# The transform along 512 first, in seven products on operands the experts share, then along 2048 in four phases

## The chip, the cores and the metric

The kernel runs on one core of a Trainium2 chip. The metric is the time of one execution on the device, in microseconds; less is better. The five engines of a core have queues of their own: TensorE (PE in the profile) multiplies matrices into eight banks of PSUM, VectorE (DVE) and GpSimd (POOL) add and subtract, ScalarE (ACT) copies, rounds and evaluates functions, SyncE (SP) issues all the DMAs.

## The reference

The result is g * a + (1 - g) * b, row by row of x (2048 rows t, 512 columns). Here a is the real part of a two-dimensional Fourier transform of x, b a mixture of all eight experts with softmax weights, and g a sigmoid of x with a weight vector.

```python
a = jnp.einsum("bsd,ed->bse", x, dft_hid_re)          # along 512
b = jnp.einsum("bsd,ed->bse", x, dft_hid_im)
y = jnp.einsum("ts,bse->bte", dft_seq_re, a) - jnp.einsum("ts,bse->bte", dft_seq_im, b)   # along 2048
...
h = _silu(xf @ w1[e]) @ w2[e]
out = out + w * h                                      # for each of 8 experts
...
return g * a + (1 - g) * b
```

The two transforms may be taken in either order.

## The kernel before

**Splitting.** Every product is computed in float32 on operands that are split into a high part, rounded by ScalarE, and a low part, the difference, made by VectorE (`vt`, L120) or GpSimd (`pt`, L117). One product of tiles is three matmuls of 128x512 (`mm`, L126, L129, L130): high by high, high by low, low by high. `split_at` plans the two steps for one tile, `wide` for a double one of 128x1024.

**Seven products.** A product of two by two blocks is made with seven block products in place of eight. Sums and differences of blocks are the operands; they are numbered 1 to 7. The transforms take them in two halves that fit PSUM: X, products 1, 2 and 5 (six banks), and Y, products 6, 3, 7 and 4 (eight banks).

**Order.** The kernel is a list of events, each with a planned time (`ev`); the list is sorted and the instructions are issued in that order on each engine. `keep_in_program_order` holds it. So what stands ahead on an engine's queue runs first, and waits for its semaphores first.

**The transform before.** It goes along 2048 first. Phases are named by (pr, c, ph): half pr of the output rows, c for the cosine or sine matrix, ph X or Y; there are eight, of NK = 8 steps k each, with 18 matmuls a step in X and 24 in Y, 1344 in all. The right operands come from the matrices (`plan_right`: tiles ca, cb and cd loaded by SP; in a Y step VectorE makes the difference cb, then two sums in ca, then the low parts c73 and c64; in an X step the difference cd and the low parts c12 and c5). The left operands xl come from x (`plan_left_x`, `plan_left_y`: some small sums and three splits per k). Finished blocks go to DRAM (ud), are loaded again, split (`plan_uv`) and multiplied with the 512-long matrices in `y_part`, four groups gi of eight times 12 matmuls, 384. The last group is interleaved with the first step of the experts. `plan_prep_x` makes the operands of the experts from x, beside this stage, and puts them into DRAM (xbd); `load_x` brings them back. The logits of the router are computed in phase (1, 0, X), with splits of their own.

**The experts.** 86 steps follow. A step has seven products m (six matmuls each, banks m_a to m_d) for the first layer and 42 for the second (banks o_a to o_d, one step later); ScalarE copies the first sums out of the bank (`snap`: tiles s, u, p) before the next product adds into the same bank. GpSimd makes the operands of w1 and w2 here.

## Time and profile before

| | us |
|---|---|
| median of three runs | 2090.86 (2092.91, 2090.86, 2090.81) |
| profiled execution, span | 2090.8 |
| TensorE busy | 2055.9 (98%) |
| VectorE busy | 1624.7 (78%) |
| GpSimd busy | 1486.9 (71%) |
| ScalarE busy | 1250.8 (60%) |

The transform takes the first 412 us of the span, the experts the rest. A page of the profile gives the busy time, a list of waits names the engine that ended each idle time, and a timeline has the single instructions. Where an engine is busy it is not shown whether it is at its own pace or is held by something else: this is read from the duration of one instruction.

### The profile page before, as it was taken

Reading aid. Unit: us, or ns where it says so; the run is one execution under the profiler, and the core shown is the slowest. Engines: PE = TensorE matmul, PEld = TensorE weight load, DVE = VectorE, ACT = ScalarE, POOL = GpSimd, SP = SyncE. Lnnn points to the kernel's source line nnn. Section 1 sums busy time; section 2 is a strip of 40 time slices with the busy share of each in tenths; the row PEclk is TensorE's granted clock in tenths of the full one; section 3 lists DMA queues with packets and bytes.
Section 4 is the critical chain, followed back from the end, with each engine's and each line's share of the span. In section 5 each row is a group of like instructions: output and inputs, shape, how many; then the busy total and the mean of one; then the engine's idle time right before and its main releaser. Section 6 shows DMA issues by size and latency. Waiting matters only on the chain.

```text
span 2090.8 us, 26671 instructions
## 1 busy us (share of the span) xinstructions
PE 2055.9 (98%) x9032; PEld 1690.9 (81%) x9032; DVE 1624.7 (78%) x2456; ACT 1250.8 (60%) x2213; POOL 1486.9 (71%) x1371
## 2 busy tenths in 40 slices
...
POOL 0010000459889888898888888888888888888884
...
DMA packets 76129, 235.65 MB, mean 113 GB/s; under 512 B 8372, under 2 KB 8372, under 8 KB 75992
## 3 DMA queue, kind: packets, MB, share of 16 engines
...
q14 instruction: 67, 0.55, 0.1%
...
## 4 chain that ended last, share of the span: by engine, by line
PE 77%; issue 2%; DMA 1%; DVE 1%; POOL 1%; ACT 1%; SPq 0%; POOLq 0%; DVEq 0%; ACTq 0%
PE o_b L126 7%; PE m_b L126 7%; PE o_b L129 7%; PE o_b L130 7%; PE m_b L129 7%; PE m_b L130 7%; PE o_d L126 4%; PE o_d L129 4%; PE o_d L130 4%; PE m_d L126 4%; PE m_d L129 4%; PE m_d L130 4%; PE o_a L129 2%; PE o_a L126 2%; PE o_a L130 2%; PE m_a L129 2%
## 5 line engine op out<-in xcount | busy, mean ns | idle before, releaser
L117 POOL TENSOR_TENSOR w<-w1s,w 128x512 fp32r<-128x512 f32 x258 | 334.7, 1297 | 137.7 <-ACT w L123 137.6
L117 POOL TENSOR_TENSOR w<-w2s,w 128x512 fp32r<-128x512 f32 (+1 forms) x264 | 335.4, 1271 | 37.1 <-ACT w L123 37.0
L120 DVE TENSOR_TENSOR acc<-o_b,acc 128x512 f32<-128x512 f32 x352 | 242.7, 690 | 118.4 <-PE o_b L130 115.7
L126 PE MATMUL m_b<-xb,w 128*128 128x512 f32 x688 | 269.3, 391 | 16.3 <-ACT xb_1w L123 8.4
L126 PE MATMUL o_b<-h,w 128*128 128x512 f32 x688 | 268.1, 390 | 1.9 <-ACT h L123 1.4
L130 PE MATMUL m_b<-xb,w 128*128 128x512 f32 x688 | 268.6, 390 | 0.0
L129 PE MATMUL m_b<-xb,w 128*128 128x512 f32 x688 | 268.6, 390 | 0.0
L129 PE MATMUL o_b<-h,w 128*128 128x512 f32 x688 | 267.7, 389 | 0.0
L130 PE MATMUL o_b<-h,w 128*128 128x512 f32 x688 | 267.7, 389 | 0.0
L123 ACT ACTIVATE w<-w1s 128x512 fp32r<-128x512 f32 x258 | 162.1, 628 | 152.1 <-POOL w1s L117 135.0
L117 POOL TENSOR_TENSOR h<-b,h 128x512 fp32r<-128x512 f32 x172 | 223.5, 1300 | 5.2 <-ACT h L123 5.2
L123 ACT ACTIVATE h<-m_c 128x512 fp32r<-128x512 f32 x172 | 103.1, 600 | 193.8 <-DVE m_c L120 191.0
L117 POOL TENSOR_TENSOR w1s<-w1s 128x256 f32<-128x256 f32 x258 | 192.0, 744 | 6.8
L126 PEld LDWEIGHTS m_b<-xb,w 128*128 128x128 f32 x688 | 129.6, 188 | 45.4 <-issue 8.8
L123 ACT ACTIVATE h<-b 128x512 fp32r<-128x512 f32 x172 | 108.7, 632 | 93.8 <-PE m_d L130 58.5
L123 ACT ACTIVATE w<-w2s 128x512 fp32r<-128x512 f32 (+1 forms) x264 | 162.4, 616 | 2.6 <-POOL w2s L117 2.6
L126 PEld LDWEIGHTS o_b<-h,w 128*128 128x128 f32 x688 | 129.2, 188 | 30.7 <-ACT h L123 1.8
L130 PEld LDWEIGHTS m_b<-xb,w 128*128 128x128 f32 x688 | 129.7, 189 | 27.1
L129 PEld LDWEIGHTS m_b<-xb,w 128*128 128x128 f32 x688 | 129.8, 189 | 26.7
L130 PEld LDWEIGHTS o_b<-h,w 128*128 128x128 f32 x688 | 129.1, 188 | 26.9
L129 PEld LDWEIGHTS o_b<-h,w 128*128 128x128 f32 x688 | 129.1, 188 | 26.5
L120 DVE TENSOR_TENSOR acc<-o_d,acc 128x512 f32<-128x512 f32 x176 | 121.1, 688 | 30.5 <-PE o_d L130 27.9
...
## 6 DMA issues: line engine op xcount, KB each, us to landing
...
```

Of the source, the lines that this page charges most:

```text
L117: pin(nc.gpsimd.tensor_tensor(*a))
L120: pin(nc.vector.tensor_tensor(*a))
L123: pin(nc.scalar.activation(dst, src, f, **kw))
L126: ins = nc.tensor.matmul(ps, lh, rh, start=start, stop=False, skip_group_check=True)
L129: nc.tensor.matmul(ps, lh, rl, start=False, stop=False, skip_group_check=True)
L130: nc.tensor.matmul(ps, ll, rh, start=False, stop=stop, skip_group_check=True)
```

## The change

The transform now goes along 512 first. **Stage one** has the seven products with the experts' own split operands of x (xop, made once, stored to xbd, and used by stage one, by the logits and by the experts) and split operands of the 512-long matrices (wop). It goes over two halves hf of the rows, seven products m in the order 1, 2, 6, 5, 7, 3, 4, four blocks j, six matmuls: 336. `evict1` puts the result into raw tiles, stored to rawd. **Stage two** goes along 2048 with cosine and sine stacked, so that there are four phases (pr, ph), (0, X), (1, X), (1, Y), (0, Y), of 16 steps each: again 1344 matmuls. The left operands come from the raw tiles, and those of the Y phases from rawd. `plan_out_x` and `plan_out_y` gate the result (`gate_y`) and put it into the experts' accumulators or to DRAM (yd); there is no `y_part` and no `plan_prep_x`. The first experts' step follows the last phase with nothing between. Loads of its x operands are planned in the last phase.

Some operations pass to GpSimd: the low parts of xop (but those of product 1), the sums of x of the second half of stage one, left_x for k from 8 on, the three sums and one low part of left_y, the first difference cb of each Y step, and gates.

VectorE in one step of a Y phase, before (names are c, then phase and step; the step is phase (0, 1, Y), k = 5):

```order
L120 TENSOR_TENSOR cb015_1252<-cb015_1252 128x512
L120 TENSOR_TENSOR ca015_1250<-cb015_1252,ca015_1250 128x512
L120 TENSOR_TENSOR ca015_1250<-ca015_1250 128x512
L120 TENSOR_TENSOR c73015l_1299<-cb015_1252,c73015h_1298 128x1024
L120 TENSOR_TENSOR c64015l_1304<-ca015_1250,c64015h_1303 128x1024
```

VectorE in one step of phase (1, Y), k = 6, after:

```order
L121 TENSOR_TENSOR ca1_6_2369<-cb1_6_2371,ca1_6_2369 128x512
L121 TENSOR_TENSOR ca1_6_2369<-ca1_6_2369 128x512
L121 TENSOR_TENSOR xl10_34_2426<-rawy10_2338,xl10_34_2426 128x512
L121 TENSOR_TENSOR c731_6l_2423<-cb1_6_2371,c731_6h_2422 128x1024
L121 TENSOR_TENSOR c641_6l_2432<-ca1_6_2369,c641_6h_2431 128x1024
```

The difference cb is gone from VectorE's step, and the low part of a left operand (xl_34) stands in it.

GpSimd in the whole of the transform before, from its setup to the experts' operands:

```order
L117 TENSOR_TENSOR c73011l_1117<-cb011_1073,c73011h_1116 128x1024
L117 TENSOR_TENSOR c64011l_1123<-ca011_1071,c64011h_1122 128x1024
L117 TENSOR_TENSOR both_81<-ident_78 18x9
L117 TENSOR_TENSOR c12101l_1449<-ca101_1410,c12101h_1448 128x1024
L117 TENSOR_TENSOR c5101_1459<-cd101_1412,c5101_1459 128x512
L117 TENSOR_TENSOR c12111l_2170<-ca111_2133,c12111h_2169 128x1024
L117 TENSOR_TENSOR c5111_2177<-cd111_2135,c5111_2177 128x512
```

GpSimd in phase (1, Y) after, around steps 5 to 7:

```order
L118 TENSOR_TENSOR cb1_5_2320<-cb1_5_2320 128x512
L118 TENSOR_TENSOR xs10_1_2408<-rawy10_2338 128x256
L118 TENSOR_TENSOR xs10_1_2408<-rawy10_2338,xs10_1_2408 128x256
L118 TENSOR_TENSOR cb1_6_2371<-cb1_6_2371 128x512
L118 TENSOR_TENSOR rawy10_2338<-rawy10_2338,xs10_1_2408 128x256
L118 TENSOR_TENSOR xl10_76_2417<-xs10_1_2408,xl10_76_2417 128x512
L118 TENSOR_TENSOR cb1_7_2412<-cb1_7_2412 128x512
```

GpSimd had single low parts at phase changes; it now has a cb in each Y step, and between these the chain xs, xs, rawy, xl_76 of a left operand.

GpSimd in stage one after, in its second half (xo are operands of x by half, product and k; xq, xa sums), where nothing stood before:

```order
L118 TENSOR_TENSOR xo1_2_0_486<-xb10_220,xo1_2_0_486 128x512
L118 TENSOR_TENSOR xo1_8_0_496<-xa10_218,xo1_8_0_496 128x512
L118 TENSOR_TENSOR xq10_503<-xb10_220,xa10_218 128x512
L118 TENSOR_TENSOR xo1_2_1_498<-xb11_221,xo1_2_1_498 128x512
L118 TENSOR_TENSOR xo1_8_1_500<-xa11_219,xo1_8_1_500 128x512
L118 TENSOR_TENSOR xq11_514<-xb11_221,xa11_219 128x512
L118 TENSOR_TENSOR xa10_218<-xa10_218 128x512
L118 TENSOR_TENSOR xa11_219<-xa11_219 128x512
L118 TENSOR_TENSOR xa10_218<-xq10_503,xa10_218 128x512
L118 TENSOR_TENSOR xa11_219<-xq11_514,xa11_219 128x512
L118 TENSOR_TENSOR xo1_6_0_561<-xa10_218,xo1_6_0_561 128x512
L118 TENSOR_TENSOR xo1_6_1_579<-xa11_219,xo1_6_1_579 128x512
```

Eight sums and two low parts stand between the low parts of product 2 and those of product 6 (the third in TensorE's order).

GpSimd after, at the start of the last phase (0, Y):

```order
L118 TENSOR_TENSOR cb0_0_2830<-cb0_0_2830 128x512
L118 TENSOR_TENSOR cb0_1_2872<-cb0_1_2872 128x512
L118 TENSOR_TENSOR c730_1l_2916<-cb0_1_2872,c730_1h_2915 128x1024
L118 TENSOR_TENSOR c640_1l_2922<-ca0_1_2870,c640_1h_2921 128x1024
L118 TENSOR_TENSOR cb0_2_2912<-cb0_2_2912 128x512
L118 TENSOR_TENSOR c211_2967<-c211_2967,gy1_2834 128x1024
L118 TENSOR_TENSOR cb0_3_2964<-cb0_3_2964 128x512
L118 TENSOR_TENSOR c121_2925<-c121_2925,gy1_2834 128x1024
L118 TENSOR_TENSOR p51_2190<-p51_2190,gy1_2834 128x1024
L118 TENSOR_TENSOR cb0_4_3007<-cb0_4_3007 128x512
```

The low parts of step 1 and three gates (c211, c121, p51) stand among the differences cb of steps 0 to 4.

TensorE where the experts begin, before: after product 1 of step 0 (m0_b) the last group of the transform (y3) follows.

```order
L126 MATMUL m0_b_3501<-xb0_1_1_3391,w1_0_12_3314 128x512
L129 MATMUL m0_b_3501<-xb0_1_1_3391,w1_0_12_3314 128x512
L130 MATMUL m0_b_3501<-xb0_1_1_3391,w1_0_12_3314 128x512
L126 MATMUL y3_0_3479<-uv3_0_1_3290,wd0_1_2368 128x512
L129 MATMUL y3_0_3479<-uv3_0_1_3290,wd0_1_2368 128x512
L130 MATMUL y3_0_3479<-uv3_0_1_3290,wd0_1_2368 128x512
```

TensorE there after:

```order
L127 MATMUL u0_41_2956<-c640_15h_3537,xl15_34_2826 128x512
L130 MATMUL u0_41_2956<-c640_15l_3538,xl15_34_2826 128x512
L131 MATMUL u0_41_2956<-c640_15h_3537,xl15_34_2826 128x512
L127 MATMUL m0_b_3605<-xb0_1_0_3207,w1_0_12_3498 128x512
L130 MATMUL m0_b_3605<-xb0_1_0_3207,w1_0_12_3498 128x512
L131 MATMUL m0_b_3605<-xb0_1_0_3207,w1_0_12_3498 128x512
L127 MATMUL m0_b_3605<-xb0_1_1_3209,w1_0_12_3498 128x512
L130 MATMUL m0_b_3605<-xb0_1_1_3209,w1_0_12_3498 128x512
L131 MATMUL m0_b_3605<-xb0_1_1_3209,w1_0_12_3498 128x512
L127 MATMUL m0_b_3605<-xb0_6_0_3250,w1_0_56_3532 128x512
```

The last matmuls of the phase (u0) are followed by product 1 and, without the y3 between, by product 6 into the same bank m0_b.

The diff, cut to its core:

```diff
-NK = NS // 2
+NK = NS
...
     gTd = dram.tile([E + 1, S], F32, name="gTd")
-    xbd = dram.tile([2, 7, 2, P, 2, GT], F32, name="xbd")
+    xbd = dram.tile([2, 8, 2, P, 2, GT], F32, name="xbd")
+    rawd = dram.tile([NK, P, 4, 256], F32, name="rawd")
...
         def load(gi, d2):
-            v[gi, d2] = stage.tile([P, 2, GT], F32, tag="stage", name=f"xr{gi}_{d2}")
-            nc.sync.dma_start(v[gi, d2], xT[d2:d2 + 2, :, gi * GT:(gi + 1) * GT]
-                              .rearrange("d p t -> p d t"))
+            hf, a = divmod(gi, 2)
+            m = ((1, 2), (8, 3))[a][d2 // 2]
+            v["w", gi, d2] = []
+            for k in range(2):
+                w = xp.tile([P, 2, GT], F32R, tag="x", name=f"xr{gi}_{d2}{k}")
+                nc.sync.dma_start(f32(w), xbd[hf, m - 1, k])
+                v["w", gi, d2].append((w[:, 0, :], w[:, 1, :]))
...
                 ev(t - 9, load, gi, d2)
-                wide(t - 2.7, t - 1.6, lambda gi=gi, d2=d2: v[gi, d2], vt,
-                     lambda w, gi=gi, d2=d2: v.__setitem__(("w", gi, d2), w), f"xs{gi}_{d2}")
                 ev(t, dots, gi, d2)
             ev(t + 2.2, copy, gi)
             ev(t + dt - 0.1, turn, gi)
...
+    def plan_w_op(m, k, t, eng):
+        r, i = lambda j: xw["r", k][:, j, :], lambda j: xw["i", k][:, j, :]
+        of = {1: lambda: r(0), 2: lambda: r(1), 7: lambda: xw["q", k], 5: lambda: i(0),
+              6: lambda: r(0), 3: lambda: r(1), 4: lambda: i(1)}
+        split_at(t, t + 0.65, lambda: xp.tile([P, 2, GT], F32R, tag="x", name=f"wo{m}_{k}"),
+                 of[m], eng, lambda w: wop.__setitem__((m, k), w), -1.0 if m in (4, 5, 6) else 1.0)
...
+    def plan_x_op(hf, m, k, t, eng):
+        a, b = lambda j: xw[hf, "a", k][:, j, :], lambda j: xw[hf, "b", k][:, j, :]
+        of = {1: lambda: a(0), 2: lambda: b(0), 7: lambda: xw[hf, "q", k], 5: lambda: a(1),
+              6: lambda: a(0), 3: lambda: b(1), 4: lambda: b(0), 8: lambda: a(1)}
+        split_at(t, t + 0.65, lambda: cp.tile([P, 2, GT], F32R, tag="w", name=f"xo{hf}_{m}_{k}"),
+                 of[m], eng, lambda w: xop.__setitem__((hf, m, k), w))
...
+    def store_x(hf, m, k):
...
+    def product1(hf, n, j):
+        m = ORDER1[n]
+        key = {2: "a", 5: "d", 3: "d"}.get(m, "b")
+        start, stop = m in (1, 2, 5), m in (2, 3, 4)
+        if start:
+            bank1[key, j] = psp.tile([P, GT], F32, tag="p", name=f"s{hf}{j}{key}")
+        for k in range(2):
+            h, w = xop[hf, m, k], wop[m, k]
+            mm(bank1[key, j], h[:, 0, sl(j)], h[:, 1, sl(j)], w[:, 0, :], w[:, 1, :],
+               start and k == 0, stop and k == 1, True)
...
+    def evict1(hf, n, j):
+        m = ORDER1[n]
+        r0, r1 = hf * 8 + 4 + j, hf * 8 + j
...
+            snap("s1", "b")
+        elif m == 2:
+            vt(half(r0, 0), bank1["a", j], tile1["s1", j], add)
+        elif m == 6:
+            snap("u2", "b")
+        elif m == 5:
+            snap("p5", "d")
+        elif m == 7:
+            vt(half(r1, 1), bank1["b", j], tile1["p5", j], add)
+        elif m == 3:
+            vt(half(r1, 0), bank1["d", j], tile1["u2", j], add)
+        else:
+            act(half(r0, 1), bank1["b", j])
+    def plan_stage1(hf, H):
+        for n, m in enumerate(ORDER1):
+            t = H + n * TM
+            if hf == 0 and n == 0:
+                ev(t, first1)
+            else:
+                for j in range(4):
+                    ev(t + j * TM / 4, product1, hf, n, j)
+            for j in range(4):
+                late = t + TM if hf == 0 and n == 0 else t + (j + 1) * TM / 4
+                ev(late + 0.3 + 0.01 * j, evict1, hf, n, j)
+            for k in range(2):
+                if n < 2:
+                    p = H + (-4.0 if n == 0 else 1.0) + 1.3 * k - (3 if hf else 0)
+                else:
+                    p = H + (n - 1) * TM - 1.0 + 2.2 * k
+                plan_x_op(hf, m, k, p, pt if n else vt)
+                ev(p + 3, store_x, hf, m, k)
+                if m == 2:
+                    q = H + 2.2 + 0.3 * k - (3 if hf else 0)
+                    plan_x_op(hf, 8, k, q, pt)
+                    ev(q + 4, store_x, hf, 8, k)
+                    plan_x_sums(hf, k, q + 0.7, H + 5 * TM - 2.5, vt if hf == 0 else pt)
+                if hf == 0:
+                    plan_w_op(m, k, p + 0.6, vt)
+                    if m == 2:
+                        plan_w_sums(k, H + 2.75 + 0.3 * k, H + 4 * TM - 2.5)
...
+    def plan_left_x(k, s, eng):
         v = {}
...
-        left_pair(s - 4.7, s - 4.0, 1, 2, k, lambda: xraw[k][:, 0:4:2, :])
-        ev(s - 3.3, s1)
-        ev(s - 2.4, hi)
-        ev(s - 0.5, lambda: vt(v["w"][:, 1, k % 2, :], v["q"], f32(v["w"][:, 0, k % 2, :]), sub))
+        ev(s, lambda: nc.sync.dma_start(rawd[k], xraw[k]))
+        left_pair(s, s + 0.7, 1, 2, k, lambda: xraw[k][:, 0:4:2, :], eng)
+        ev(s + 0.2, s1)
...
+        def load():
+            xraw[k] = xp.tile([P, 4, 256], F32, tag="x", name=f"rawy{k}")
+            nc.sync.dma_start(xraw[k], rawd[k])
         def s3():
-            v["q"] = tmp.tile([P, 2, 256], F32, tag="c", name=f"xq{k}_1")
-            vt(v["q"][:, 0, :], xraw[k][:, 0, :], xraw[k][:, 1, :], sub)
+            v["q"] = tmp.tile([P, 2, 256], F32, tag="c", name=f"xs{k}_1")
+            pt(v["q"][:, 0, :], xraw[k][:, 0, :], xraw[k][:, 1, :], sub)
+        ev(s - 7, load)
         ev(s, s3)
-        ev(s + 0.5, lambda: vt(v["q"][:, 1, :], xraw[k][:, 3, :], v["q"][:, 0, :], sub))
-        ev(s + 1.0, lambda: vt(xraw[k][:, 2, :], xraw[k][:, 2, :], v["q"][:, 1, :], sub))
-        left_pair(s + 1.0, s + 2.0, 7, 6, k, lambda: v["q"])
-        left_pair(s + 1.7, s + 3.2, 3, 4, k, lambda: xraw[k][:, 2:4, :])
+        ev(s + 0.8, lambda: pt(v["q"][:, 1, :], xraw[k][:, 3, :], v["q"][:, 0, :], sub))
+        ev(s + 1.6, lambda: pt(xraw[k][:, 2, :], xraw[k][:, 2, :], v["q"][:, 1, :], sub))
+        left_pair(s + 1.7, s + 2.4, 7, 6, k, lambda: v["q"], pt)
+        left_pair(s + 2.5, s + 3.2, 3, 4, k, lambda: xraw[k][:, 2:4, :], vt)
...
-        ev(t, lambda: vt(v["b"][:, 0, :], v["b"][:, 1, :], v["b"][:, 0, :], sub))
+        ev(t - 0.6, lambda: pt(v["b"][:, 0, :], v["b"][:, 1, :], v["b"][:, 0, :], sub))
         ev(t + 0.65, lambda: vt(v["a"][:, 0, :], v["b"][:, 0, :], v["a"][:, 0, :], add))
         if lo is None:
             wide(t + 0.7, t + 2.0, lambda: v["b"], eng, keepb, f"c73{nm}")
...
+    def gate_y(hf, t, i, a, eng):
+        eng(t, t, gy[hf][:, a, None, :].to_broadcast([P, 2, GT]), OP.mult)
+        if hf:
+            nc.sync.dma_start(yd[i, a], t)
+        else:
+            acc[hf, i, a] = t
...
+        if pr:
+            ev(te - 14, gate_y_row, 1, xp, "x")
+            ev(te + 2, lambda: gate_y(1, v["c11"], 0, 0, pt))
...
+            ev(te - 22, lambda: gate_y(0, v["c11"], 0, 0, pt))
+        else:
+            ev(te - 14, gate_y_row, 1, gp, "g")
...
+        geng = pt if pr else vt
+        ev(t + 7.5, lambda: vt(v["c12"], v["c12"], v["p5"], add))
+        ev(t + 8.8, lambda: vt(v["p5"], v["p5"], v["s1"], add))
+        ev(t + 9.0, lambda: gate_y(pr, v["c21"], 1, 0, geng))
+        ev(t + 10.0, lambda: gate_y(pr, v["c12"], 0, 1, geng))
+        ev(t + 11.0, lambda: gate_y(pr, v["p5"], 1, 1, geng))
...
-    phases = ((0, 0, "X"), (0, 1, "X"), (0, 0, "Y"), (0, 1, "Y"), (1, 0, "X"), (1, 0, "Y"),
-              (1, 1, "X"), (1, 1, "Y"))
...
+    plan_stage1(0, 0.0)
+    plan_stage1(1, T1 / 2)
+    for k in range(8):
+        plan_left_x(k, T1 / 2 + 1.0 + 4.4 * k, vt)
+        plan_left_x(8 + k, T1 + 0.9 + 4.4 * k, pt)
+    phases = ((0, "X"), (1, "X"), (1, "Y"), (0, "Y"))
+    T, before = T1, None
+    for pr, ph in phases:
+        dt = TY if ph == "Y" else TX if pr else TX0
...
+            t = s - (6.8 if ph == "X" else 8.3)
+            if before == "Y" and k == 1:
+                plan_right(pr, ph, k, t - 7, T - 4.0, r, pt, T - 2.1)
             else:
-                t = s - (6.8 if ph == "X" else 8.3)
-                if before == "Y" and k == 1:
-                    plan_right(pr, c, ph, k, t - 7, T - 4.0, r, pt, T - 2.1)
-                else:
-                    if before == "Y" and k == 2:
-                        t = T + 3.4
-                    plan_right(pr, c, ph, k, t - 7, t, r)
-            ev(s, dft, pr, c, k, (1, 2, 5) if ph == "X" else (6, 3, 7, 4), r, ps)
-        at = lambda k, o=0.0: T + k * dt + o
-        if first:
...
+        if (pr, ph) == (0, "X"):
+            plan_logits(T + 6.0, 8.0)
+        if (pr, ph) == (1, "X"):
...
+            for k in range(NK):
+                plan_left_y(k, T - 4 + 9.2 * k)
...
-    for gi in range(NG - 1):
-        for n in range(8):
-            ev(T + 2.72 * n, y_part, gi, n)
...
-        if gi == 0:
-            plan_prep_x(0, 0, T + 7, 1.9, vt)
-            plan_prep_x(0, 1, T + 21.5, 1.9, pt)
...
-    base[0] = T + 2.72
-    for n in range(8):
-        ev((n - 1) * 2.72 + 1.36, y_part, NG - 1, n)
-    for q in range(4):
-        ev(6 * 2.72 + 1.37, y_out, NG - 1, q)
+    base[0] = T
...
-        ev(-9, load_x, 0, m)
+        ev(-TY * (10 - n), load_x, 0, m)
...
```

## Rows read from the trace of the kernel before

**Rows 1.** The page, busy time of TensorE with the others, and GpSimd's busy share in 40 slices of the span (tenths).
```profile
PE 2055.9 (98%) x9032; PEld 1690.9 (81%) x9032; DVE 1624.7 (78%) x2456; ACT 1250.8 (60%) x2213; POOL 1486.9 (71%) x1371
...
POOL 0010000459889888898888888888888888888884
```

**Rows 2.** TensorE's waits up to 490 us: tile waited with, releasing engine and tile: us in total, times, longest.
```profile
PE u L126 <- ACT c12000h L123: 8.9, 1, 8.9
PE m_b L126 <- ACT xb_1w L123: 8.4, 1, 8.4
PE m_b L126 <- ACT s L123: 4.4, 3, 1.7
PE m_b L126 <- ACT u L123: 3.6, 1, 3.6
...
PE ln L180 <- ACT ls L123: 0.7, 1, 0.7
PE u L129 <- DVE c64113l L120: 0.6, 1, 0.6
PE u L126 <- DVE c L120: 0.6, 2, 0.3
PE u L129 <- DVE c12007l L120: 0.3, 1, 0.3
```

**Rows 3.** TensorE's timeline in the last full-rate stretch of the transform, first and last of 84 matmuls: start us, duration us, engine, line, operation.
```profile
385.15 0.39 PE L126 MATMUL y<-uv,wd 128*128 128x512 f32 x1
...
403.96 0.39 PE L130 MATMUL y<-uv,wd 128*128 128x512 f32 x1
```

**Rows 4.** TensorE's timeline where the transform gives way to the experts (in brackets: idle time before, and its releaser).
```profile
412.74 0.77 PE L126 MATMUL m_b<-xb,w 128*128 128x512 f32 x1 [8.39 <-ACT xb_1w L123]
...
415.85 0.40 PE L129 MATMUL y<-uv,wd 128*128 128x512 f32 x1
...
430.40 0.39 PE L130 MATMUL y<-uv,wd 128*128 128x512 f32 x1
434.38 0.79 PE L126 MATMUL m_b<-xb,w 128*128 128x512 f32 x1 [3.59 <-ACT u L123]
...
439.66 0.42 PE L126 MATMUL y<-uv,wd 128*128 128x512 f32 x1
...
449.55 0.39 PE L126 MATMUL m_b<-xb,w 128*128 128x512 f32 x1
```

**Rows 5.** Timelines of VectorE (DVE) and GpSimd (POOL) at three places, VectorE first at each: 122 us, 163 us, 398 us. A row with x2 or more holds that many operations.
```profile
122.52 1.28 DVE L120 TENSOR_TENSOR s<-u,s 128x512 f32<-128x512 f32 x2
...
123.44 2.41 POOL L117 TENSOR_TENSOR c73011l<-cb,c73011h 128x1024 fp32r<-128x1024 f32 x1 [122.14 <-PE u L129]
...
163.23 2.88 DVE L120 TENSOR_TENSOR cd<-cd,ca 128x512 f32<-128x512 f32 x1
...
162.87 2.69 POOL L117 TENSOR_TENSOR c12101l<-ca,c12101h 128x1024 fp32r<-128x1024 f32 x1 [34.06 <-ACT wgs L123]
...
398.85 1.36 DVE L468 SCALAR_TENSOR_TENSOR uv<-us,uv 128x512 fp32r<-128x512 f32 x1 [0.35 <-ACT uv L123]
400.13 1.22 DVE L120 TENSOR_TENSOR xt<-b,b 128x512 f32<-128x512 f32 x1
402.03 2.73 DVE L468 SCALAR_TENSOR_TENSOR uv<-us,uv 128x512 fp32r<-128x512 f32 x2 [0.67 <-ACT uv L123]
...
398.37 1.29 POOL L117 TENSOR_TENSOR xb_1w<-b,xb_1w 128x512 fp32r<-128x512 f32 x1 [5.09 <-ACT xb_1w L123]
399.62 1.18 POOL L117 TENSOR_TENSOR w1s<-w1s 128x256 f32<-128x256 f32 x1
400.77 1.74 POOL L117 TENSOR_TENSOR xb_1w<-b,xb_1w 128x512 fp32r<-128x512 f32 x1
402.47 1.73 POOL L117 TENSOR_TENSOR w<-w1s,w 128x512 fp32r<-128x512 f32 x1
```

**Rows 6.** Groups of like instructions, VectorE to 404 us and GpSimd to 480 us: line, engine, operation, shapes, count | busy us, mean ns of one | idle time before.
```profile
L120 DVE TENSOR_TENSOR ca<-cb,ca 128x512 f32<-128x512 f32 x32 | 22.1, 692 | 1.0
...
L120 DVE TENSOR_TENSOR c12011l<-ca,c12011h 128x1024 fp32r<-128x1024 f32 x1 | 1.2, 1227 | 0.0
...
L117 POOL TENSOR_TENSOR w<-w2s,w 128x256 fp32r<-128x256 f32 x6 | 4.5, 744 | 1.4 <-ACT w L123 1.4
...
L117 POOL TENSOR_TENSOR c<-cd,c 128x512 fp32r<-128x512 f32 x2 | 2.6, 1304 | 2.6 <-ACT c L123 2.6
...
L117 POOL TENSOR_TENSOR c64011l<-ca,c64011h 128x1024 fp32r<-128x1024 f32 x1 | 2.4, 2391 | 0.0
```

**Rows 7.** Timelines of TensorE and of ScalarE (ACT) at the start.
```profile
8.90 0.79 PE L126 MATMUL u<-c12000h,xl 128*128 128x512 f32 x1 [8.90 <-ACT c12000h L123]
...
17.54 0.39 PE L126 MATMUL u<-c12001h,xl 128*128 128x512 f32 x1
...
4.28 1.28 ACT L123 ACT_TABLE_LOAD   x1 [4.28 <-DMA xr<-x_dram]
...
14.97 1.06 ACT L123 ACTIVATE c12002h<-ca 128x1024 fp32r<-128x1024 f32 x1 [0.33 <-DMA ca<-cT_dram]
```

**Rows 8.** Stretches of 5 us with the busy time of each engine; the last numbers are the granted clock, the DMA share and the GB/s moved.
```profile
10.00:15.00 5.00, 3.97 (x9) 3.14 (x10) 5.00 (x8) 3.69 (x7) 0.00 (x0) 1.00 1.04 409
...
30.00:35.00 5.00, 5.00 (x23) 4.13 (x22) 5.00 (x10) 3.93 (x7) 0.00 (x0) 1.00 1.03 386
```

More of the change, by code (lines that the diff above doesn't have):

```diff
@@ new lines, in first1 @@
+    def first1():
+        for j in range(4):
+            bank1["b", j] = psp.tile([P, GT], F32, tag="p", name=f"s0{j}b")
+        for k in range(2):
+            h, w = xop[0, 1, k], wop[1, k]
+            for p, (a, b) in enumerate(((0, 0), (1, 0), (0, 1))):
+                for j in range(4):
+                    ins = nc.tensor.matmul(bank1["b", j], h[:, a, sl(j)], w[:, b, :],
+                                           start=k == 0 and p == 0, stop=False, skip_group_check=True)
+                    if j == 0:
+                        pin(ins)
@@ new lines, in evict1, with raw, half, snap @@
+    def evict1(hf, n, j):
+        m = ORDER1[n]
+        r0, r1 = hf * 8 + 4 + j, hf * 8 + j
+        def raw(r):
+            if r not in xraw:
+                xraw[r] = xp.tile([P, 4, 256], F32, tag="x", name=f"raw{r}")
+            return xraw[r]
+        def half(r, h):
+            return raw(r)[:, 2 * h:2 * h + 2, :].rearrange("p a d -> p (a d)")
+        def snap(key, b):
+            if key != "p5":
+                t = tmp.tile([P, GT], F32, tag="c", name=f"{key}{hf}{j}")
+            else:
+                if j % 2 == 0:
+                    tile1["pair"] = gp.tile([P, 2, GT], F32, tag="g", name=f"p5{hf}{j}")
+                t = tile1["pair"][:, j % 2, :]
+            tile1[key, j] = t
+            act(t, bank1[b, j])
+        if m == 1:
+            snap("s1", "b")
[11 more added lines that the diff above has]
+            act(half(r0, 1), bank1["b", j])
```

279 lines of the change are left out of this document (115 added, 164 removed).

## The prediction

> **What bounds the kernel now.** I read the busy lines first: TensorE is busy 98% of the span, and GpSimd has next to nothing to do in the first sixth [rows 1]. So the time is TensorE's matmuls plus its stops. The list of TensorE's waits up to 490 us holds nearly all of them [rows 2]: 8.9 us before the first matmul, 8.4 and 3.6 us where the transform gives way to the experts, 4.4 us in three waits for copies of the experts' first sums, and some 2.2 us at changes of phase. The rest is the pace: 84 matmuls from 385.15 to 403.96 have 83 intervals, 18.81 / 83 = 0.2266 us each [rows 3]. After a stop the clock is at its lower level (1.2 GHz), with 0.425 us from matmul to matmul (412.74 to 415.85; the second stop's 434.38 to 439.66 is 12 matmuls in 5.28 us, 2.56 more than at full pace) [rows 4]. The profiled span is 2090.8 us and the median of the runs 2090.86, so the sum below is made against 2090.8 and needs no correction.
>
> **A fact of the trace that decides the rest.** A GpSimd operation and a VectorE operation that both take two inputs from SBUF run one after the other. VectorE's 128x512 subtraction at 163.23 took 2.88 us beside GpSimd's 128x1024 from 162.87, which ended at 165.56; VectorE ended at 166.11, 0.55 us later [rows 5]. The VectorE additions at 122.52, of which one input is in PSUM, took 1.28 for two beside the GpSimd one at 123.44: undisturbed. The chain from 398.37 shows both orders: GpSimd's 128x512 takes 1.73, its 128x256 1.18, VectorE's 512 takes 1.36 to 1.37 [rows 5]; each is the sum of two holds, 0.55 for VectorE 512, 1.17 for GpSimd 512, 0.62 for GpSimd 256. So 1.1 for VectorE 1024 and 2.3 for GpSimd 1024 (162.87's 2.69 less what VectorE still held). Alone they take 0.69, 1.30, 0.74, 1.23 and 2.39 [rows 6]. Before, GpSimd has only seven operations ahead of the experts' operands, so this costs little.
> The Trainium skill, "SBUF — State Buffer", section "SBUF: two separate sides", says that VectorE with two SBUF inputs and a GpSimd operation that reads SBUF take one shared port pair as an exclusive lock for the whole instruction; the trace agrees (2.88 against 0.69 us), and the rule speaks against handing VectorE's work to GpSimd in phases where VectorE is nearly full. Were the two only side by side at their durations alone, (e), (g) and (h) below would be near nothing and the sum that of rival 1.
>
> **The change part by part.**
> (a) Matmuls. Stage one is 2 x 7 x 4 x 6 = 336 where 384 stood; the 2048-long stage stays at 1344. 48 x 0.2266 = -10.9 us, all on the path. The order confirms it (48 fewer rows on TensorE), so that the change does less work is no open question.
> (b) From the transform to the experts. Before, 404.19 (403.96 and one pace) to 449.55 is 45.36 us, with 96 + 42 matmuls in it, 31.27 us; 14.1 are lost, and with the 4.4 of the later copies 18.5 [rows 2, 3, 4]. After, the operands come out of DRAM, loaded during the last phase, and 8.4 and 3.6 go. But step 0's 42 matmuls now stand without the interleaved 96: 9.5 us of TensorE against VectorE's 17 operations of step 0 (0.6 each) and five 128x1024 ones with two SBUF inputs (two sums, three gates; 1.1 each), 15.7 us. I give step 0 2.5 us of stops, step 1's first copy, which ScalarE has behind step 0's chain, most of the 15.7 - 9.5 - 2.5 = 3.7 that are left, 3.4, a lower clock after it 2.5, and the later copies 1.4 and 1.2: 11.0. So -7.5; -18.5 if nothing waits, 0 if the serial chain of step 0 costs as much again.
> (c) Four phases for eight: half of the 2.2 us at phase changes, -1.
> (d) The start. Before, TensorE starts at 8.90 and its 19th matmul at 17.54, where 18 at full pace are 4.08: 13.5 us lost [rows 7]. After, the first matmul needs two pieces of 256 KB and not three transfers, so I take 5.5 us (the first landing, 4.28, and a split). But the second product's k = 1 half waits for a split that VectorE has behind a sum (wq1) of the fourth and the fifteenth load. Fifteen pieces are 3.93 MB; before, 3.67 MB are in at 14.97 [rows 7], at some 0.4 MB per us (386 to 409 GB/s, [rows 8]) 15.6. Five operations of 0.6 and locks against four GpSimd ones make the split's end some 20; the third product waits again. 72 matmuls (16.3 us) end at about 33.2, 16.9 lost: +3.4 (0 to +8).
> (e) Stage one, second half. The sums and low parts of its operands are twelve GpSimd operations of 128x512, 12 x 1.27 = 15.2 us [rows 6], between buffers that come free after the first half and the third product, which has two products of 24 matmuls ahead of it (10.9 us). +4.6 (0 to +8; 0 if they start early).
> (f) First two phases (X): VectorE 2.18 us of holds per step of 4.08 and GpSimd's left operands 1.56 (3.58 every 9.2 us): 3.74 below 4.08, +0.5. The added stores and loads (the first stage's result, and the experts' operands in place of x) are hidden: 54.9 MB up to the end of the first X phase at 0.4 MB per us are 137 us, TensorE needs 150.
> The skill's same page, in the table of section "A bandwidth-pool intuition that's wrong (but worth ruling out)", has 358 GB/s between HBM and a core; by it those transfers would take 153 us and the start be some 3 us worse. The rows show 386 to 409 [rows 8], so the measurement decides.
> (g) Phase (1, Y). Per step: VectorE two of 512 and two of 1024, 2 x 0.55 + 2 x 1.1 = 3.3; GpSimd the difference cb that was VectorE's, 1.17; 16 steps 71.5 us. The left operands, 3 x 0.62 + 1.17 + 0.55 = 3.58 each, half of them (8) in this phase: 28.6. The first gate 2.3. Sum 102.4 us through one port against 16 x 5.44 = 87 for TensorE: 15.4 late, less the one step or so of stock that the operand buffers hold at the start: +14. Lower bound 0 (GpSimd's operations all find gaps: then VectorE's own 3.8 per step at 1.23 and 0.69, as before, is below 5.44), upper 25 (every stop brings the lower clock).
> (h) Phase (0, Y). A Y phase fills all eight banks, so its first matmuls wait for the evictions of the one before: 2. Step 1's two low parts (2.3 each) and three gates (2.3 each) are on GpSimd, with five cb, 17.4; VectorE beside them 4 steps' 1024s, 5 steps' 512s and two sums, 16.5. Less step 0's share (4.4), 29.5 against four steps' 21.8: +7.7. At the end the experts' first w1 operations and a gate are on GpSimd ahead of the last step's cb: some 1. Together +10 (0 to +13).
> **Sum**: -10.9 - 7.5 - 1 + 3.4 + 4.6 + 0.5 + 14 + 10 = +13.1: **2104 us**.
>
> **Rivals.**
> 1. The locks are absorbed: faster. If the sums of (e), (g), (h) do not reach TensorE (operands made ahead, as GpSimd is idle early), 2090.8 - 10.9 - 7.5 - 1 + 3.4 = 2075. It decides when a Y step's holds stay below 5.44: without the left operands 4.47, with them 6.4, so it needs these to be done almost wholly in the phase before. For it: GpSimd's idle time [rows 1]. Against it: the order puts them at one per 9.2 us. 0.17.
> 2. Half of it is absorbed, and the gains and losses cancel: +4.6 + 14 + 10 halved to 14.3 makes -1.7, 2089. 0.18.
> 3. Each late step of the Y phases stops TensorE long enough to bring the lower clock, as the 3.59 us stop did (2.5 us each [rows 4]): seven such stops, +17, 2121. For it: stops of one to four us are what (h) makes. Against it: the 0.3 to 0.7 us waits of [rows 2] left the pace as it was. 0.10.
> That the start is bound by transfers is the smaller case of (d), inside the range.
>
> **How the numbers follow.** The forecast has 0.55, rivals 0.17, 0.18 and 0.10. About 0.2% (4.2 us) is what a measurement can tell from no change: 2086.7 to 2095.0 is the same. Faster: rival 1 and a fifth of rival 2, 0.20. Same: two thirds of rival 2 and a tenth of the forecast, 0.18. Slower: the rest, 0.62. The range leaves out rival 1 and the worst of rival 3: 2083 to 2122, from the bounds of (b), (g) and (h); its lower end takes in rival 2.
>
> **What would show it.** (a): 48 fewer matmuls. (b): no wait for xb, one for a copy s of some 3 us. (d), (e): waits of the first stage for wo and xo. (g), (h): waits of TensorE for c73 or c64 in the last two phases, 20 us and more, with VectorE's ca and c64 groups at means well over 0.69 and 1.23. The prediction is wrong if these phases run at 5.44 us per step although the means grow (rival 1), or if the clock row shows long low stretches in them (rival 3).

## The result and the profile after

| | us |
|---|---|
| before, median (4 runs) | 2091.46 (2090.81 to 2092.91) |
| after, median (4 runs) | 2103.93 (2102.27 to 2104.45) |
| after / before | 1.0055, 95% interval 1.0041 to 1.0069 |
| profiled execution after, span | 2102.1 (before 2090.8) |

The change made the kernel slower by 12.5 us in the medians and 11.3 in the spans. The page after, busy times and GpSimd's slices, against [rows 1]:

```profile
PE 2055.4 (98%) x8984; PEld 1685.7 (80%) x8984; DVE 1648.4 (78%) x2356; ACT 1256.8 (60%) x2240; POOL 1682.9 (80%) x1507
...
POOL 4624776378888889888888898888988888889884
```

TensorE has 48 fewer matmuls (8984 records for 9032) and is busy for the same share. GpSimd is busy from the first slice on. TensorE's waits up to 490 us, the longest, against [rows 2]:

```profile
PE s00b L323 <- ACT wo L124: 6.0, 1, 6.0
PE m_b L127 <- ACT s L124: 5.1, 3, 3.2
PE s00a L130 <- DVE wo L121: 3.9, 1, 3.9
PE u L130 <- DVE c_3l L121: 3.3, 2, 1.6
PE m_d L127 <- ACT p L124: 2.7, 1, 2.7
PE u L127 <- DVE s L121: 2.4, 1, 2.4
PE u L130 <- DVE c_6l L121: 2.2, 1, 2.2
PE u L130 <- DVE c_11l L121: 2.1, 1, 2.1
PE u L130 <- DVE c_15l L121: 1.9, 2, 1.1
```

The two long waits for xb and u are gone. In their place stands a row of waits of the transform for VectorE's low parts c (c_3l is step 3's, of one phase or the other). The timeline of TensorE gives the ends of the stages:

```profile
5.96 0.79 PE L323 MATMUL s00b<-wo,xo 128*128 128x512 f32 x1 [5.96 <-ACT wo L124]
...
20.30 0.80 PE L130 MATMUL s00a<-wo,xo 128*128 128x512 f32 x1 [3.95 <-DVE wo L121]
...
54.71 0.39 PE L127 MATMUL s10b<-wo,xo 128*128 128x512 f32 x1
...
96.94 0.39 PE L127 MATMUL u<-c_0h,xl 128*128 128x512 f32 x1
...
241.38 0.39 PE L127 MATMUL u<-c_0h,xl 128*128 128x512 f32 x1
...
347.59 0.39 PE L131 MATMUL u<-c_15h,xl 128*128 128x512 f32 x1
350.35 0.47 PE L127 MATMUL u<-c_0h,xl 128*128 128x512 f32 x1 [2.37 <-DVE s L121]
...
444.85 0.39 PE L127 MATMUL m_b<-xb,w 128*128 128x512 f32 x1
...
458.31 0.39 PE L127 MATMUL m_b<-xb,w 128*128 128x512 f32 x1
...
463.02 0.50 PE L127 MATMUL m_b<-xb,w 128*128 128x512 f32 x1 [3.19 <-ACT s L124]
```

Stage one's first half ends at 54.71, the second at 96.94; (0, X) and (1, X) end at 241.38, (1, Y) at 347.82 (347.59 and one pace), (0, Y) at 444.85, step 0 of the experts at 458.31. From each stretch its matmuls of 128x512 times the pace, 0.2266 us [rows 3], are taken; what is left counts as lost. Before, the same sums give 13.5 us to the 19th matmul (17.54), 18.15 from there to 404.19, and 16.8 from 404.19 to 449.55. The 18.15 and the 13.9 of the X phases after hold the router's 80 small matmuls too (L168 to L218 before, L177 to L225 after), which are work and no stops: 13.6 us before, 12.8 after.

| term of the prediction | forecast | measured |
|---|---|---|
| (a) 48 matmuls | -10.9 | -10.9 |
| (b) to the experts and their first steps | -7.5 | -10.3 (3.9 for 16.8; from there to the end 1643.8 for 1641.3) |
| (c), (f) changes of phase, X phases | -0.5 | -4.3 (13.9 for 18.15) |
| (d) first half of stage one | +3.4 | +3.2 (16.64 for 13.46) |
| (e) second half | +4.6 | +4.2 (42.23 less 168 x 0.2266) |
| (g) phase (1, Y) | +14 | +19.4 (106.44 less 384 x 0.2266) |
| (h) phase (0, Y), with the wait at its start | +10 | +10.0 (97.03 less 384 x 0.2266) |
| sum | +13.1 | +11.3 |

VectorE first and GpSimd behind it in phase (1, Y), as [rows 5]:

```profile
260.47 1.75 DVE L121 TENSOR_TENSOR c_3l<-ca,c_3h 128x1024 fp32r<-128x1024 f32 x1
262.14 1.22 DVE L121 TENSOR_TENSOR ca<-cb,ca 128x512 f32<-128x512 f32 x1
263.39 1.65 DVE L121 TENSOR_TENSOR ca<-ca 128x512 f32<-128x512 f32 x1
264.97 2.30 DVE L121 TENSOR_TENSOR c_4l<-cb,c_4h 128x1024 fp32r<-128x1024 f32 x1
...
262.77 1.72 POOL L118 TENSOR_TENSOR xl<-xs,xl 128x512 fp32r<-128x512 f32 x1
264.46 1.72 POOL L118 TENSOR_TENSOR cb<-cb 128x512 f32<-128x512 f32 x1
```

VectorE's 128x1024 took 1.75 and 2.30 us where it takes 1.23 alone [rows 6], its 128x512 1.22 and 1.65 for 0.69, and GpSimd's 128x512 took 1.72 for 1.30. The two groups of VectorE's sums, from 245 to 335 us (count | busy us, mean ns of one | idle before):

```profile
L121 DVE TENSOR_TENSOR ca<-cb,ca 128x512 f32<-128x512 f32 x13 | 14.8, 1142 | 3.5 <-POOL cb L118 3.5
L121 DVE TENSOR_TENSOR ca<-ca 128x512 f32<-128x512 f32 x13 | 14.4, 1109 | 0.4
```

The means of 1.14 and 1.11 us stand where 0.69 was. So VectorE looks busy, but a part of its time is waiting that no list of waits shows: it is in the durations.

### The profile page after: what moved, and what is told of

The parts are those of the page before. It is cut to its first block, busy times and chain, and to the rows that moved or that the text cites. A ratio compares the mean times of both kernels' runs of the same rounds, so it can differ in the third digit from the quotient of the medians.

```text
span 2102.1 us, 26673 instructions
## 1 busy us (share of the span) xinstructions
PE 2055.4 (98%) x8984; PEld 1685.7 (80%) x8984; DVE 1648.4 (78%) x2356; ACT 1256.8 (60%) x2240; POOL 1682.9 (80%) x1507
## 4 chain that ended last, share of the span: by engine, by line
PE 87%; POOL 3%; DVE 3%; issue 3%; DMA 2%; ACT 1%; SPq 0%; POOLq 0%; ACTq 0%; DVEq 0%
PE o_b L127 7%; PE o_b L131 7%; PE o_b L130 7%; PE m_b L127 7%; PE m_b L131 7%; PE m_b L130 7%; PE o_d L127 4%; PE o_d L131 4%; PE o_d L130 4%; PE m_d L127 4%; PE m_d L131 4%; PE m_d L130 4%; PE u L130 3%; PE u L131 3%; PE u L127 3%
## 5 line engine op out<-in xcount | busy, mean ns | idle before, releaser
L121 DVE TENSOR_TENSOR acc<-o_b,acc 128x512 f32<-128x512 f32 x176 | 121.4, 690 | 59.0 <-PE o_b L131 57.6
L127 PE MATMUL m_d<-xb,w 128*128 128x512 f32 x344 | 133.9, 389 | 2.7 <-ACT p L124 2.7
```

The costliest lines, as they stand in the source:

```text
L121: pin(nc.vector.tensor_tensor(*a))
L127: ins = nc.tensor.matmul(ps, lh, rh, start=start, stop=False, skip_group_check=True)
```

## The experiments

Each run gives its median, its ratio to the kernel before on the same chip, and what a stage lost, worked out as above from one profiled execution. The changed kernel has 2103.93, ratio 1.0055. Stages that no edit touched differ from profile to profile: the first half of stage one lost 15.8 to 17.0 us, the second 3.2 to 6.1. A difference within that says nothing.

**1. The difference cb back on VectorE.**

```diff
-        ev(t - 0.6, lambda: pt(v["b"][:, 0, :], v["b"][:, 1, :], v["b"][:, 0, :], sub))
+        ev(t, lambda: vt(v["b"][:, 0, :], v["b"][:, 1, :], v["b"][:, 0, :], sub))
```

> The first difference cb of every Y step goes back from GpSimd to VectorE; all else as in the changed kernel. Theory (one operation with two SBUF inputs at a time on VectorE and GpSimd together): each cb then holds 0.55 us instead of 1.17, so phase (1, Y) needs 102.4 - 16 x 0.62 = 92.5 us of holds and its 19 us of lateness fall to about 9; with what (0, Y) gets back, 10 to 13 us less than 2104, about 2092. Rival (GpSimd as such is late, its queue and the waits on ScalarE): a cb no longer queues behind left operands, the same sign but all lateness of (1, Y) would go, 17 to 20 us less, about 2086, and VectorE's operations would keep means near those of GpSimd-free stretches.

Measured: 2092.4 us, ratio to before 1.0004 (0.9995 to 1.0013). Phase (1, Y) with the wait behind it lost 13.2 us for 21.9, (0, Y) 6.8 for 7.5. (1, Y) alone fell from 19.4 to 11.3, and VectorE's sums ca from 245 to 335 us to 0.84 us each, still over 0.69. The theory's number came out, and lateness stayed as it said; the rival's number did not come.

**2. The left operands of the Y phases on VectorE.** Cb stays GpSimd's.

```diff
-            pt(v["q"][:, 0, :], xraw[k][:, 0, :], xraw[k][:, 1, :], sub)
+            vt(v["q"][:, 0, :], xraw[k][:, 0, :], xraw[k][:, 1, :], sub)
...
-        left_pair(s + 1.7, s + 2.4, 7, 6, k, lambda: v["q"], pt)
+        left_pair(s + 1.0, s + 2.0, 7, 6, k, lambda: v["q"], vt)
```

> The three small sums and the low part of xl_76 of each left operand of the Y phases go from GpSimd to VectorE; cb stays on GpSimd. Theory of the serial holds: a left operand then holds 3 x 0.29 + 2 x 0.55 = 1.97 us instead of 3.58; (1, Y) needs 71.5 + 8 x 1.97 + 2.3 = 89.6 us of holds against 87 of TensorE, so of 19 us of lateness some 3 to 5 stay: about 2089. Rival (VectorE is simply full): VectorE has 2.3 us more work per 9.2 us, 3.7 + 1.35 = 5.05 us per step of 5.44, no gain or a loss, 2104 or above.

Measured: 2094.29 us, 1.0011 (1.0002 to 1.0020). VectorE got more work, and the kernel became 9.6 us faster: that VectorE is merely full is out. But 10.0 us of (1, Y)'s 19.4 stayed (12.6 with the wait behind), not 3 to 5. VectorE was busy 88.2 of the 90 us from 245 on. Its operations of 128x512, 128x1024 and 128x256 follow each other 0.60, 1.14 and 0.34 us apart from start to start in this trace, a little more than the holds (0.55, 1.1, 0.29). Summed by this pace, sixteen steps take 16 x (2 x 0.60 + 2 x 1.14 + 1.17) = 74.4 us, eight left operands 8 x 2.2 = 17.8 and the gate 2.3: 94.5 against 87.0, 7.5 late. So that the pace is longer than the holds is a part of why the size was too low; the other 2.5 us stay open.

**3 and 4. More GpSimd work that nothing waits for, with and without reads.** Steps 4 to 13 of (0, Y), where TensorE had no wait from 373 to 438 us. The added operations write a spare tile and change no result.

```diff
+        if pr == 0 and 4 <= k <= 13:
+            for n in range(6):
+                ev(t - 0.59, lambda: pin(nc.gpsimd.tensor_tensor(ident, ident, ident, OP.mult)))
```

In run 4 it is `range(10)` and `nc.gpsimd.memset(ident, 0.0)`.

> Steps 4 to 13 of phase (0, Y) get six more GpSimd operations each, products of a spare 128x128 tile with itself, some 2 us in all, that nothing waits for. GpSimd has 1.3 us of work per 5.44 there and TensorE no waits. Serial holds: 4.47 + 2.0 = 6.5 us per step against 5.44, so ten steps are late by some 8 to 10 us: about 2113. Rival (GpSimd's own time or queue matters): 3.3 us of 5.44, nothing is late, 2104.

> As the run with the additional products, but with ten memsets of the same tile in each step, some 2 us of GpSimd that read nothing from SBUF. Serial holds among operations that read: no change, 2104. If any GpSimd work beside VectorE costs, or GpSimd's queue, it is as slow as the other run, about 2113.

Measured: 2115.09 us (1.0109, 1.0095 to 1.0123) with the products, 2105.51 (1.0066, 1.0052 to 1.0081) with the memsets. The first is the forecast number for another reason. GpSimd's timeline there:

```profile
389.65 1.30 POOL L118 TENSOR_TENSOR cb<-cb 128x512 f32<-128x512 f32 x1
390.90 5.26 POOL L495 TENSOR_TENSOR ident<-ident 128x128 f32<-128x128 f32 x6
396.12 1.29 POOL L118 TENSOR_TENSOR cb<-cb 128x512 f32<-128x512 f32 x1
```

Six products took 5.26 us, not 2; with cb they fill 6.5 us of GpSimd per step, more than TensorE's 5.44, and cb itself is late. So run 3 does not tell the theories apart. The memsets, 2.6 us per step with the gaps between them, left (0, Y) at 7.2 us lost for 7.5 (the profile is of the fastest of five executions, 2101.6).

**5. Two reading additions of known length instead.**

```diff
+            for n in range(2):
+                ev(t - 0.59, lambda: pt(tmp.tile([P, GT], F32, tag="c", name=f"dm{nm}"),
+                                        v["b"][:, 0, :], v["b"][:, 1, :], add))
```

> The spare products of the earlier run took 0.83 us each and filled GpSimd's own queue, so that run does not tell the two theories apart. Here steps 4 to 13 of phase (0, Y) get two more GpSimd additions of 128x512 each, from two inputs in SBUF, that nothing waits for: 2.5 us alone, with cb 3.8 of 5.44, near the 2.6 us of the memsets. Serial holds: 4.47 + 2 x 1.17 = 6.8 us per step, ten steps late by 1.37 each, less a step's stock: 11 to 13 us more, about 2116, with the mean of VectorE's ca and c64 well up. Rival (only GpSimd's own time counts): as with the memsets, 2104 to 2106.

Measured: 2120.25 us (1.0130, 1.0115 to 1.0145), (0, Y) lost 24.4. Groups of GpSimd and VectorE from 385 to 430 us, first with the memsets (run 4), then here:

```profile
L495 POOL MEMSET ident<- 128x128 f32 x70 | 14.3, 205 | 3.6
...
L121 DVE TENSOR_TENSOR ca<-cb,ca 128x512 f32<-128x512 f32 x8 | 6.0, 750 | 4.3 <-POOL cb L118 4.3
L121 DVE TENSOR_TENSOR ca<-ca 128x512 f32<-128x512 f32 x8 | 6.0, 744 | 0.3
```

```profile
L118 POOL TENSOR_TENSOR dm<-cb 128x512 f32<-128x512 f32 x14 | 25.3, 1828 | 0.6
...
L121 DVE TENSOR_TENSOR ca<-ca 128x512 f32<-128x512 f32 x7 | 10.7, 1522 | 0.2
L121 DVE TENSOR_TENSOR ca<-cb,ca 128x512 f32<-128x512 f32 x7 | 10.2, 1460 | 0.0
```

With some 2.6 us of GpSimd per step that does not read, the two ca stay at 0.75 and 0.74 us (1.02 and 0.75 in the changed kernel in this stretch), and TensorE is busy for all 45 us; with the reading additions ca is at 1.46 and 1.52, twice its own length, GpSimd's additions are at 1.83 for 1.30, and TensorE is busy 38.9 of 45 us. It is the reading, not GpSimd's time. The Trainium skill, "SBUF — State Buffer", section "Who interferes with whom", states that VectorE with two SBUF inputs contends with a GpSimd instruction that reads SBUF and not with one that only writes it; the two runs agree. The price was more than the sum of holds: a step took 7.84 us (ca to ca, 388.83 to 396.67), not 6.8; where the last 1.0 us comes from is open.

**6. The start, in another order.** The operands of product 2 are planned 0.4 us apart, not 1.3.

```diff
-                    p = H + (-4.0 if n == 0 else 1.0) + 1.3 * k - (3 if hf else 0)
+                    p = H + (-4.0 if n == 0 else 1.0) + (1.3 if n == 0 or hf else 0.4) * k - (3 if hf else 0)
```

> In the first half of stage one the operands of product 2 are planned 0.4 us apart instead of 1.3, so that VectorE makes the low part wo2_1 ahead of the sums wq that wait for the fifteenth load. Theory (the order on VectorE, not the loads, holds the second product): its second half starts at about 14 to 15 us instead of 20.3, the third product waits for the last loads instead, and 168 matmuls end 3 to 6 us earlier: about 2099. Rival (the loads bound the start): the wait moves to the third product whole, no change, 2104.

Measured: 2104.2 us (1.0056, 1.0041 to 1.0071). The wait at 20.30 went, and product 6 then waited 4.1 us:

```profile
23.21 0.50 PE L127 MATMUL s00b<-wo,xo 128*128 128x512 f32 x1 [4.12 <-ACT s L124]
```

The first half lost 17.1 for 16.6, at the upper end of the scatter: no gain. The rival's number came, and the wait moved as it said; but behind the last load VectorE still had its sums to make, so that the loads alone hold the start is not shown.

**7. The sums of the second half on VectorE.**

```diff
-                    plan_x_sums(hf, k, q + 0.7, H + 5 * TM - 2.5, vt if hf == 0 else pt)
+                    plan_x_sums(hf, k, q + 0.7, H + 5 * TM - 2.5, vt)
```

> The eight sums of x for the second half of stage one go from GpSimd to VectorE. Theory (a chain of twelve GpSimd operations of 1.27 us ahead of the third product): the chain is four long, its waits of about 4 us go, 2100. Rival (buffers free too late, or VectorE full there): the wait stays under another name, 2104.

Measured: 2099.99 us (1.0031, 1.0018 to 1.0044). The second half lost 0.01 us for 4.16 (3.2 to 6.1 in the runs without this edit).

**8. Cb and left operands on VectorE, the latter earlier.** Edits 1 and 2, and

```diff
-                plan_left_y(k, T - 4 + 9.2 * k)
+                plan_left_y(k, T - 4 + 5.8 * k if k < 12 else T + 68 + 14 * (k - 12))
```

> cb and the left operands of the Y phases both on VectorE, and the left operands every 5.8 us in phase (1, X) (twelve of sixteen) and every 14 us after. No GpSimd operation but the gates stands beside VectorE then: (1, X) 5.8 us hold 1.42 x 2.34 + 2.3 = 5.6 of VectorE's pace, (1, Y) 4.08 of 5.44 and 2.3 per 14 us. Theory: of the 19 us of (1, Y) at most 4 stay, (0, Y) loses 6 to 8 instead of 10: about 2086. Rival (VectorE full, or buffers short for early left operands): TensorE waits in (1, X) instead, 2092 as with cb alone or above.

Measured: 2084.1 us (0.9954, 0.9939 to 0.9969). (1, Y) lost 4.4 us, (0, Y) 4.6, (1, X) no more than before (2.0). VectorE's sums from 245 to 335 us, against the same groups above:

```profile
L121 DVE TENSOR_TENSOR ca<-cb,ca 128x512 f32<-128x512 f32 x17 | 11.7, 691 | 0.5
L121 DVE TENSOR_TENSOR ca<-ca 128x512 f32<-128x512 f32 x17 | 11.7, 690 | 0.4
```

They are back at their own 0.69.

**9. The start again.** Edit 6, and the sums of k = 0 ahead of those of k = 1.

```diff
-                    plan_x_sums(hf, k, q + 0.7, H + 5 * TM - 2.5, vt if hf == 0 else pt)
+                    plan_x_sums(hf, k, q + 0.7 + (0 if hf else 1.9 * k), H + 5 * TM - 2.5, vt if hf == 0 else pt)
...
-                        plan_w_sums(k, H + 2.75 + 0.3 * k, H + 4 * TM - 2.5)
+                        plan_w_sums(k, H + 2.75 + 2.2 * k, H + 4 * TM - 2.5)
```

> On the changed kernel alone, the start once more: besides the low part wo2_1 ahead of the sums, VectorE makes the six sums of k = 0, whose loads are in by 13 us, before it waits with wq1 for the fifteenth load at 16. Theory (with both the order on VectorE is what held the third product until 23 to 26 us): product 6 starts at about 19.6, when product 2 is done, and the first half of stage one ends 3 to 4 us earlier: about 2100. Rival (the sixteenth load and the sums of k = 1 behind it end last anyway): the wait moves to the second half of product 6, under 1.5 us gained, 2103.

Measured: 2104.56 us (1.0062, 1.0046 to 1.0077). TensorE at the start, then GpSimd:

```profile
20.45 0.50 PE L127 MATMUL s00b<-wo,xo 128*128 128x512 f32 x1 [1.58 <-ACT s L124]
...
24.13 0.80 PE L131 MATMUL s00b<-wo,xo 128*128 128x512 f32 x1 [2.44 <-POOL xo L118]
...
19.47 7.53 POOL L118 TENSOR_TENSOR xo<-xa,xo 128x512 fp32r<-128x512 f32 x3 [3.70 <-ACT xo L124]
```

Product 6 began at 20.45, 2.8 us sooner than in run 6, and then waited for its second half, for GpSimd's low parts (three in 7.5 us, held by VectorE's sums) and VectorE's; the first half lost 15.9 us for 16.6, within the scatter. VectorE had no idle time from 10.93 to 23.5. So in neither order is there a gain; that it is VectorE's work of sums and splits that holds the start fits this, but no run had less of that work.

**10 to 12. All together.** Run 10 is run 8 with edit 7, the gates on VectorE and those of the last phase put off; run 11 adds edit 9; run 12 is run 10 with two of the last phase's gates on GpSimd and the sums and one gate back in place.

```diff
-        geng = pt if pr else vt
+        late = (12, 18, 7.4, 13, 19) if pr else (26, 30, 33, 27, 31)
-        ev(t + 7.5, lambda: vt(v["c12"], v["c12"], v["p5"], add))
+        ev(t + late[0], lambda: vt(v["c12"], v["c12"], v["p5"], add))
...
-        ev(t + 9.0, lambda: gate_y(pr, v["c21"], 1, 0, geng))
+        ev(t + late[2], lambda: gate_y(pr, v["c21"], 1, 0, vt))
```

In run 12 the second list is (7.5, 8.8, 7.4, 10, 26) and c21's and p5's gates are `pt`.

> As the run with cb and the left operands on VectorE (2084), with the sums of the second half of stage one on VectorE too, and all gates of the transform's result on VectorE: those of the third phase spread over four steps of the last, those of the last phase put off until the experts' second step. Theory (a GpSimd gate holds VectorE for 2.3 us; in step 0 VectorE's five wide operations make TensorE wait): stage one gives back 4 to 6 us, (0, Y) 2, the experts' first steps 3: about 2074. Rival (VectorE is at its limit in (1, Y) and the start of (0, Y)): only stage one gives back, 2079 or more.

> As the run before with the order of the start changed as well (low part wo2_1 first, the sums of k = 0 ahead of those of k = 1). The gains are at different places and should add: 3 to 4 us below it, about 2071; if the start is bound by its loads, the same as it.

> As the run with late gates, but the end of the transform otherwise: there the late sums and gates moved TensorE's waits into the experts' steps 1 and 2, where they cost some 5 us more than in place. Here the sums and the gate of c12 are back in step 0 on VectorE, and the gates of c21 (at once) and of p5 (in step 1) are GpSimd's. VectorE's operations of the experts have an input in PSUM, so by the theory GpSimd's gates do not hold them; step 0 has three wide VectorE operations for five: 2071 to 2073. Rival (any GpSimd gate costs TensorE its 2.4 us, by holding VectorE or by delaying the operands of w1 on GpSimd): 2076 or more.

Measured: 2077.18 us (0.9930, 0.9917 to 0.9944), 2076.88 (0.9929, 0.9916 to 0.9941), 2077.45 (0.9924, 0.9911 to 0.9938). In run 10 the transform ends at 414.24 us for 426.15 in run 8; stage one's second half and (0, Y) lose 0.02 us or less each, (1, Y) 2.9. But the experts' part took 4.7 us longer (1660.8 from there to the end, for 1656.1): with the sums and gates out of step 0, TensorE's waits for copies up to step 1's first were 5.3 us, as in run 8 (5.1), and behind the sums and gates put off, which VectorE now has from 434 to 446 us, it waited 2.7 and 2.8, for 1.5 in run 8. Run 11 shows again that the start's order is worth nothing. Run 12 missed its 2071 to 2073 and came out at its rival's 2076 or more. GpSimd there, then VectorE, ScalarE and TensorE:

```profile
418.66 2.39 POOL L118 TENSOR_TENSOR c<-c,gy 128x1024 f32<-128x1024 f32 x1
421.01 1.71 POOL L118 TENSOR_TENSOR w1s<-w1s 128x256 f32<-128x256 f32 x1
...
419.59 0.70 DVE L121 TENSOR_TENSOR m_a<-m_a,s 128x512 f32<-128x512 f32 x1 [2.05 <-PE m_a L131]
...
422.75 0.63 ACT L124 ACTIVATE w<-w1s 128x512 fp32r<-128x512 f32 x1 [3.99 <-POOL w1s L118]
423.40 1.28 ACT L124 ACT_TABLE_LOAD   x1
...
427.20 0.79 PE L127 MATMUL m_d<-xb,w 128*128 128x512 f32 x1 [4.99 <-ACT p L124]
```

The gate (c by gy) on GpSimd put the operands of w1 behind it back; ScalarE waited 4.0 us for one, had a table to load behind it, and TensorE waited 5.0 for the copy p. VectorE's operation with a PSUM input beside that gate took its usual 0.70 us (at 419.59), so as the theory says it was not held; the cost came through GpSimd's queue. Run 10 with the end of run 8, by these parts an estimated 2072 to 2073, was not run.

## Why the prediction was right

The forecast was 2104 and the measured median 2103.93. That the number is so close is in part luck: (g) was forecast 5 us too small, the gains of (b) and (c) together nearly 7 too small.

- The deciding step, one operation at a time when both engines read two inputs from SBUF, holds. It was tested from five sides: taking cb away gave 11.5 us, taking the left operands away 9.6, both and an earlier schedule 19.8; added reads cost 16.3 us, added memsets of like length 1.6, within what the runs scatter (2101.6 to 2108.6). These are differences of medians from several chips; by the ratios to before they are 10.7, 9.2, 21.1, 15.7 and 2.3 us.
- (g): the mechanism was right and the size too small, 14 for 19.4. The forecast was the sum of holds; by VectorE's pace as in run 2 the same sum is 74.4 + 8 x 3.63 + 2.3 = 105.7 us, 18.7 late, less a step's stock. In the changed kernel's (1, Y) there were also 23 matmuls at the lower clock, about 4.6 us; whether these add to VectorE's lateness or lie within it is open.
- The sign named for (g) and (h), waits for c73 or c64 of 20 us and more, came with some 16 us. The rest of the 29.4 lost is the 2.4 us wait for s, the lower clock (6 us in the two phases) and what each stop costs beyond the idle time listed.
- (h): 10.0 for 10 in sum (the parts as forecast make 10.7), but not part by part: the start cost 2.5 us for 2, the waits for the low parts of steps 2 and 3 4.0 for 7.7, the end 1.3 for 1, and the lower clock after the start 1.6, which had no term. Run 10, with cb, left operands and gates on VectorE and the gates spread, took it to zero; step 1's two low parts stayed on GpSimd there.
- (e): the chain of twelve GpSimd operations is the cause; run 7 leaves four of them, and the loss is gone whole.
- (d): the size was right and the reason only half. The wait for wo2_1 came at 20.30, where the forecast put it. But taking it away gained nothing: two orders without it were no faster (runs 6 and 9). What was late next, VectorE's sums and GpSimd's low parts for product 6, was not asked there.
- (b): the stretch of before was counted with 96 matmuls of the interleaved group; its first twelve ran ahead of 404.19, so 84 remain, and before lost 16.8 us there, not 14.1. After, step 0's stops cost 3.9 us for 2.5, step 1's copy 3.2 for 3.4, and the lower clock behind it 1.4 (seven matmuls) for 2.5.
- (c): the list of waits before has 2.2 us at changes of phase, but each stop costs more than the idle time that is listed (42.03 to 42.73 is 0.47 over the pace, listed 0.32). Without the router's matmuls, what stands over the pace fell from 4.0 to 0.8 us, most of the 4.3 gained; another 0.8 is the router's own time.
- Rival 1, locks absorbed, had its place only when the schedule was changed: run 8 does what it asked for, the left operands almost wholly in the phase before, and has them and cb away from GpSimd. Rival 2, half of (e), (g) and (h) absorbed, did not come: the three measured 33.6 us for 28.6. Rival 3's long low stretches of the clock did not come; four short ones did, three in (1, Y) and one in (0, Y), 31 matmuls and some 6 us for its 17.
- Two readings of the prediction are off without effect: in (f) 3.58 us every 9.2 are 1.59 per step and not 1.56, and VectorE's 1.36 in [rows 5] is the rest of a GpSimd hold and its own, not two whole holds.
